# A DiT block on one core: four instead of five groups of scale columns, two of them placed inside their K step, and batch 1's layer-norm statistics swapped between two engines

## The chip, the cores and the metric

The kernel runs on one core of one Trainium2 chip. The metric is device microseconds of one execution, the median of several. Names used: PE is TensorE, DVE is VectorE, ACT is ScalarE, POOL is GpSimd, SP is the engine that issues most loads.

## The reference

Shapes are B = 2, N = 256, D = 1152 and F = 4608, all in bf16.

```python
mod = (silu(c) @ w_mod).reshape(B, 6, 1, D)
shift_a, scale_a, gate_a, shift_m, scale_m, gate_m = [mod[:, i] for i in range(6)]
h = layernorm(x) * (1 + scale_a) + shift_a
q, k, v = split(h @ wqkv)                       # 2 heads of 576
a = softmax(q k^T / sqrt(576)) v @ wo
x = x + gate_a * a
h2 = layernorm(x) * (1 + scale_m) + shift_m
out = x + gate_m * (gelu(h2 @ w_fc1) @ w_fc2)
```

The change touches only the first part: the first layer norm, its scale, and the K projection.

## The kernel before

**Tiles.** The 512 tokens are four tiles of 128 (0 and 1 are batch 0, 2 and 3 are batch 1). D is nine chunks of 128. All weights are loaded once into wide tiles by SP, in the order in which they are used. The instructions of each engine run in the order in which the program writes them: the end of the kernel adds a dependency from each instruction to the one before it on its engine. Eight semaphores are shared in turn by the loads, so that a load waits until the eighth load before it has landed.

**Layer norm of x.** For tiles 1 and 3, DVE computes mean and variance (`stats_piece`, L193 and L195, in three pieces of 384 columns). For tiles 0 and 2, ACT does (`act_stats`, L204: two passes over the tile that sum and sum squares), and small operations on DVE and POOL make mean and variance of the sums (`act_sq_mean` L211, `act_var` L222, `act_mean` L216). The reciprocal root comes from POOL (`pool_rsqrt`, L327) for tiles 0, 1 and 3, and from ACT (`ln_exp_rsqrt`, L227 and L228: Ln, then Exp with scale -0.5) for tile 2. `norm1` (L231, DVE) subtracts and multiplies into `xn`, first columns 0 to 512 (`CUT`), later the rest.

**Chunks and scale.** PE transposes `xn` chunk by chunk into PSUM (`transpose_x`, L262, tile `pt`). `scale_group(k0, k1)` (L245) makes the scales of the chunks k0 to k1 with nine matmuls a chunk of two columns each, out of `w_scale_a`. `scale_add` (L255 on DVE, L253 on ACT) adds 1 and puts them in SBUF. `modulate` multiplies half a chunk (one batch) by its scale and writes it to SBUF, on DVE (L268) or ACT (L270); `both` has DVE do batch 0 and ACT batch 1. Chunk 0 of batch 0 is modulated by L356 with the scale straight from PSUM.

**K projection.** `k_step(k)` (L278) runs chunk k of h against six column blocks of `w_k` (m from 0 to 5), each into its own PSUM bank; with `c0, c1` on one batch alone, with `m0, m1` on some of the blocks. The steps 0 to 2 are done by halves, with the preparation of the next chunks between them. From step 3 on, the loop is

```python
for k in range(3, KD):
    if k in (3, 5, 7):
        k1 = min(k + 3, KD)
        scale_add(scale_group(k + 1, k1), k + 1, k1)
    if k < KD - 1:
        both(transpose_x([k + 1], range(NT)), k + 1)
    k_step(k)
```

After it come the last three column blocks (`k_panel`, L307), the shift, Q, attention, the output projection and the MLP, none of which changes. `warm` (L173) and `fill` (L321) are matmuls on zeros that nothing reads.

**Loads.** `SGROUPS` names the groups of scale columns. SP loads x in four loads (tiles 0, 1, 3, 2: L86), then for each group its scale columns (L107) and the rows of `w_k` for the same chunks (L104), and then the other columns of `w_k`, the shift columns and the rest.

Of the kernel before, what the change touches and what calls it, by code (L numbers as in the profile page):

```python
# [9 lines left out]
BF16 = mybir.dt.bfloat16  # L10
ACT = mybir.ActivationFunctionType
# [4 lines left out]
LN_EPS = 1e-5  # L16
# [3 lines left out]
def kernel(  # L20
# [11 lines left out]
    nc = tc.nc  # L32
    B, N, D = x.shape
# [3 lines left out]
    P = 128  # L37
    T = B * N
    NT = T // P
    TPB = N // P  # L40
    KD = D // P
# [18 lines left out]
    def acc_tile(shape, name, dt=FP32):  # L60
        return psum.tile(shape, dt, name=name, tag="acc", bufs=6)

    def aux_tile(shape, name, dt=FP32):
        return psum.tile(shape, dt, name=name, tag="aux", bufs=2)
# [27 lines left out]
    eps_t = const.tile([P, 1], FP32, name="eps_t")  # L92
# [2 lines left out]
    sT = act.tile([P, KD, SW], BF16, name="sT")  # L95
    nc.gpsimd.memset(sT[:], 0.0)

    SGROUPS = [(0, 2), (2, 4), (4, 6), (6, 8), (8, 9)]
    KM1 = 6
    w_scale_a = wide_tile("w_scale_a")  # L100
    w_k = wide_tile("w_k")
# [1 line left out]
    def load_k(k0, k1, c0, c1):  # L103
        nc.sync.dma_start(w_k[:, k0:k1, c0:c1], wqkv_v[:, k0:k1, D + c0:D + c1])  # L104

    for k0, k1 in SGROUPS:
        nc.sync.dma_start(  # L107
            w_scale_a[:, :, k0 * P:k1 * P],
            wmod_v[:, :, S_SCALE_A * D + k0 * P:S_SCALE_A * D + k1 * P],
        )  # L110
        for a, z in [(0, 1), (1, 2)] if k0 == 0 else [(k0, k1)]:
            load_k(a, z, 0, KM1 * P)
    load_k(0, KD, KM1 * P, D)

    first_load = {}
# [29 lines left out]
    hT0 = aT  # L145
# [41 lines left out]
    mv1 = small.tile([P, NT, 2], FP32, name="mv1", tag="mv1", bufs=1)  # L187
    rstd1 = small.tile([P, NT], FP32, name="rstd1", tag="rstd1", bufs=1)
# [3 lines left out]
    def stats_piece(t, j):  # L192
        nc.vector.bn_stats(stats1[t][:, j, :], x_sb[:, t, j * PW:(j + 1) * PW])  # L193
        if j == NPD - 1:
            nc.vector.bn_aggr(mv1[:, t, :], stats1[t][:].rearrange("p a b -> p (a b)"))  # L195
# [3 lines left out]
    dsq = small.tile([P, NT], FP32, name="dsq", tag="dsq", bufs=1)  # L199
    dm2 = small.tile([P, NT], FP32, name="dm2", tag="dm2", bufs=1)  # L200

    def act_stats(t):
        for f, dst in ((ACT.Identity, dsum), (ACT.Square, dsq)):
            nc.scalar.activation(  # L204
                xns[t][:], x_sb[:, t, :], f, bias=x_sb[:, t, 0:1], scale=-1.0,
                accum_out=dst[:, t:t + 1],
            )

    def act_sq_mean(t):
        one = slice(t, t + 1)  # L210
        nc.vector.scalar_tensor_tensor(  # L211
            dm2[:, one], dsum[:, one], -1.0 / (D * D), dsum[:, one], op0=ALU.mult, op1=ALU.mult
        )

    def act_mean(t):
        nc.gpsimd.tensor_scalar(  # L216
            mv1[:, t, 0:1], dsum[:, t:t + 1], -1.0 / D, x_sb[:, t, 0:1], op0=ALU.mult, op1=ALU.add
        )

    def act_var(t):  # L220
        one = slice(t, t + 1)
        nc.vector.scalar_tensor_tensor(  # L222
            mv1[:, t, 1:2], dsq[:, one], 1.0 / D, dm2[:, one], op0=ALU.mult, op1=ALU.add
        )

    def ln_exp_rsqrt(dst, var):
        nc.scalar.activation(dst, var, ACT.Ln, bias=eps_t[:], scale=1.0)  # L227
        nc.scalar.activation(dst, dst, ACT.Exp, scale=-0.5)  # L228

    def norm1(t, c0, c1):  # L230
        nc.vector.tensor_scalar(  # L231
            xns[t][:, c0:c1], x_sb[:, t, c0:c1], mv1[:, t, 0:1], rstd1[:, t:t + 1],
            op0=ALU.subtract, op1=ALU.mult,
        )


    scale_a = act.tile([P, KD, B], FP32, name="scale_a")

    def scale_group(k0, k1, tile_of=aux_tile):
        pm = tile_of([P, k1 - k0, B], "pm")  # L240
        for j in range(k0, k1):
            if j == 0:
                nc.tensor.matmul(pm[:, 0, :], ones_row[:], ones_row[:, 0:B], start=True, stop=False)
            for k in range(KD):
                nc.tensor.matmul(  # L245
                    pm[:, j - k0, :], w_scale_a[:, k, j * P:(j + 1) * P], sT[:, k, 0:B],
                    start=(k == 0 and j > 0), stop=(k == KD - 1),
                )
        return pm

    def scale_add(pm, k0, k1, eng="d"):
        if eng == "a":
            nc.scalar.activation(scale_a[:, k0:k1, :], pm[:], ACT.Identity, bias=ones[:])  # L253
        else:
            nc.vector.tensor_scalar_add(scale_a[:, k0:k1, :], pm[:], 1.0)  # L255

    def transpose_x(ks, ts, pt=None, j0=0):
        if pt is None:
            pt = aux_tile([P, len(ks), len(ts) * P], "pt", BF16)
        for j, t in enumerate(ts, j0):  # L260
            for i, k in enumerate(ks):
                nc.tensor.transpose(pt[:, i, j * P:(j + 1) * P], xns[t][:, k * P:(k + 1) * P], ident[:])  # L262
        return pt

    def modulate(pt, i, k, b, j0, eng):
        dst, src, sc = hT0[:, k, b * N:(b + 1) * N], pt[:, i, j0:j0 + N], scale_a[:, k, b:b + 1]
        if eng == "d":
            nc.vector.tensor_scalar_mul(dst, src, sc)  # L268
        else:
            nc.scalar.mul(dst, src, sc)  # L270
# [3 lines left out]
    def k_step(k, c0=0, c1=T, m0=0, m1=KM1):  # L274
        for m in range(m0, m1):
            if k == 0 and c0 == 0:
                pk[m] = acc_tile([P, T], "pk")
            nc.tensor.matmul(  # L278
                pk[m][:, c0:c1], w_k[:, k, m * P:(m + 1) * P], hT0[:, k, c0:c1],
                start=(k == 0 and c0 == 0), stop=(k == KD - 1), skip_group_check=True,  # L280
            )
# [31 lines left out]
    BT = [range(b * TPB, (b + 1) * TPB) for b in range(B)]  # L313

    def both(pt, k):
        for b, e in enumerate("da"):
            modulate(pt, 0, k, b, b * N, e)

    def fill(n):
        for _ in range(n):  # L320
            nc.tensor.matmul(pwarm[:], zeros[:, 0:P], zeros[:], start=True, stop=True)  # L321

    def pool_eps(t):
        nc.gpsimd.tensor_scalar_add(mv1[:, t, 1:2], mv1[:, t, 1:2], LN_EPS)

    def pool_rsqrt(t0, t1):
        nc.gpsimd.tensor_tensor(  # L327
            rstd1[:, t0:t1], mv1[:, t0:t1, 1:2].rearrange("p t o -> p (t o)"),
            neg_half[:, 0:t1 - t0], op=ALU.pow,
        )  # L330

    warm(8, pwarm)
    act_stats(0)
    act_stats(2)
    for j in range(NPD):
        stats_piece(1, j)
    act_sq_mean(0)
    nc.gpsimd.tensor_scalar_add(dm2[:, 0:1], dm2[:, 0:1], LN_EPS)
    pool_eps(1)
    stats_piece(3, 0)  # L340
    act_var(0)
    pool_rsqrt(0, 2)
    act_mean(0)
    stats_piece(3, 1)
    stats_piece(3, 2)
    pool_eps(3)
    pool_rsqrt(3, 4)
    norm1(1, 0, CUT)
    norm1(0, 0, CUT)
    pt_a = transpose_x([0, 1], BT[0])  # L350
    act_sq_mean(2)
    act_mean(2)
    norm1(3, 0, CUT)
    pm0, pm1 = [scale_group(k, k + 1, acc_tile) for k in range(2)]
    act_var(2)
    nc.vector.tensor_scalar_mul(hT0[:, 0, 0:N], pt_a[:, 0, :], pm0[:, 0, 0:1])  # L356
    scale_add(pm1, 1, 2, "a")
    modulate(pt_a, 1, 1, 0, 0, "d")
    ln_exp_rsqrt(rstd1[:, 2:3], mv1[:, 2, 1:2])
    nc.scalar.copy(scale_a[:, 0:1, :], pm0[:])  # L360
    norm1(2, 0, CUT)
    fill(1)
    pt_c = aux_tile([P, 2, N], "pt", BF16)
    transpose_x([0, 1], [3], pt_c, 1)
    fill(1)
    k_step(0, 0, N)
    transpose_x([0, 1], [2], pt_c, 0)
    k_step(1, 0, N)
    modulate(pt_c, 0, 0, 1, 0, "d")
    modulate(pt_c, 1, 1, 1, 0, "a")  # L370
# [13 lines left out]
    norm1(3, CUT, D)  # L384
    k_step(2, 0, N)
    k_step(2, N, T)
    for k in range(3, KD):
        if k in (3, 5, 7):
            k1 = min(k + 3, KD)
            scale_add(scale_group(k + 1, k1), k + 1, k1)  # L390
        if k < KD - 1:
            both(transpose_x([k + 1], range(NT)), k + 1)
        k_step(k)
    for m in range(KM1):
        k_evac(m)

# [446 lines left out]
```

## Time and profile before

| | |
|---|---|
| median of 9 runs | 243.92 us (243.48 to 244.48) |
| the profiled execution | 243.75 us, its span 242.0 us |
| PE busy | 236.5 us (98% of the span), 1691 instructions |
| DVE, ACT, POOL busy | 91.4, 59.5 and 28.9 us |
| HBM read | 50.14 MB |
| granted PE clock | full in all slices |
| K step matmuls (L278) | 70 in the trace, 12.9 us |
| scale matmuls (L245) | 81, the first at 9.6 us, the last at 23.1 us |

The page splits the span into 40 slices; PE is busy to nine tenths or more in all but the first two and the last. A chain of waits that is followed back from the last instruction tells which engine's time sets the end. The timeline lists instructions by start and duration, with the idle time before them and what ended it in brackets; matmuls of one line are merged, so that a row "x18" covers eighteen of them. A few matmul records are missing from a trace.

### The profile page before, as it was taken

Reading aid. Unit: us, or ns where it says so; the run is one execution under the profiler, and the core shown is the slowest. Engines: PE = TensorE matmul, PEld = TensorE weight load, DVE = VectorE, ACT = ScalarE, POOL = GpSimd, SP = SyncE. Lnnn points to the kernel's source line nnn. Section 1 sums busy time; section 2 is a strip of 40 time slices with the busy share of each in tenths; the row PEclk is TensorE's granted clock in tenths of the full one; section 3 lists DMA queues with packets and bytes.
Section 4 is the critical chain, followed back from the end, with each engine's and each line's share of the span. In section 5 each row is a group of like instructions: output and inputs, shape, how many; then the busy total and the mean of one; then the engine's idle time right before and its main releaser. Section 6 shows DMA issues by size and latency. Waiting matters only on the chain.

```text
span 242.0 us, 3989 instructions
## 1 busy us (share of the span) xinstructions
PE 236.5 (98%) x1691; PEld 145.3 (60%) x1701; DVE 91.4 (38%) x193; ACT 59.5 (25%) x120; POOL 28.9 (12%) x48
## 2 busy tenths in 40 slices
PE   8899999999999999999999999999999999999994
PEld 5685444466667665888844444444665666566674
DVE  4642442319325678831002999950010000000001
ACT  6632322307215032671422333322000000000000
POOL 2400000001400323200000000001121111111111
PEclk9999999999999999999999999999999999999999
DMA  6999999997599999239999999999200000000000
GB/s 213 327 315 285 377 366 392 389 392 246 105 318 395 390 374 148 48 60 359 389 392 392 340 327 284 276 327 282 98 16 16 20 16 16 20 16 18 29 21 16
DMA packets 48781, 53.29 MB, mean 220 GB/s; under 512 B 9587, under 2 KB 36475, under 8 KB 48763
## 3 DMA queue, kind: packets, MB, share of 16 engines
q1 hardware_dynamic: 41312, 50.14, 62.4%
q10 hardware_dynamic: 6939, 1.71, 4.9%
q0 software_dynamic: 512, 1.19, 1.8%
q8 instruction: 13, 0.21, 0.4%
q14 instruction: 5, 0.04, 0.1%
HBM read 50.14 MB, written 1.19 MB: 212 GB/s over the span
## 4 chain that ended last, share of the span: by engine, by line
PE 94%; DMA 3%; SPq 1%; issue 0%; DVE 0%; ACT 0%; DVEq 0%; ACTq 0%
PE pacc L788 29%; PE pacc L732 29%; PE pacc L679 7%; PE pacc L588 7%; PE pq L510 7%; PE pk L278 5%; DMA w_scale_a<-in_w_mod_dram 3%; PE pk L307 2%; PE pa L628 2%; PE ps_s L545 2%; PE pn L405 2%; PE pm L245 1%; PE pt L262 1%; SPq L86 1%; PE pg L487 0%
## 5 line engine op out<-in xcount | busy, mean ns | idle before, releaser
L732 PE MATMUL pacc<-hT,w_f 128*128 128x256 bf16 (+1 forms) x427 | 70.3, 325 | 0.3
L788 PE MATMUL pacc<-w_f,gT 128*128 128x384 bf16 (+2 forms) x468 | 70.5, 314 | 0.0
L788 PEld LDWEIGHTS <-gT 128*128 128x128 bf16 x468 | 44.4, 98 | 26.2
L732 PEld LDWEIGHTS <-w_f 128*128 128x128 bf16 x432 | 42.2, 98 | 27.6
L794 DVE TENSOR_TENSOR tmp<-pacc,gate 128x384 f32<-128x384 f32 (+2 forms) x13 | 6.9, 527 | 65.6 <-PE pacc L788 57.4
L764 ACT ACTIVATE gT<-pacc 128x512 bf16<-128x512 f32 x24 | 14.3, 597 | 32.7 <-PE pacc L732 32.7
L458 DVE SCALAR_TENSOR_TENSOR part<-w_gate_m,s,part 128x1152 f32<-128x1152 bf16 x16 | 21.4, 1414 | 0.0
L796 POOL TENSOR_TENSOR o_sb<-tmp,x 128x384 bf16<-128x384 f32 (+1 forms) x12 | 11.6, 970 | 54.0 <-DVE tmp L794 54.0
L679 PE MATMUL pacc<-w_o,big 128*128 128x384 bf16 x108 | 17.9, 326 | 0.0
L510 PE MATMUL pq<-hT,w_q 128*128 128x512 bf16 x79 | 17.7, 379 | 0.1
L588 PE MATMUL pacc<-w_v,hT 128*128 128x384 bf16 x108 | 17.7, 326 | 0.0
L588 PEld LDWEIGHTS <-hT 128*128 128x128 bf16 x108 | 10.5, 98 | 7.1 <-issue 0.3
L679 PEld LDWEIGHTS <-big 128*128 128x128 bf16 x108 | 10.4, 98 | 7.2 <-issue 0.4
L510 PEld LDWEIGHTS <-w_q 128*128 128x128 bf16 x81 | 7.9, 98 | 9.4
L278 PE MATMUL pk<-big,w_k 128*128 128x256 bf16 (+1 forms) x70 | 12.9, 324 | 0.1
L685 POOL TENSOR_TENSOR x<-tmp,x_sb 128x384 f32<-128x384 f32 x8 | 7.3, 912 | 26.8 <-DVE tmp L684 26.8
L456 DVE TENSOR_SCALAR part<-w_gate_m,s 128x1152 f32<-128x1152 bf16 x2 | 1.6, 818 | 22.1 <-DMA w_gate_m<-in_w_mod_dram 22.1
L480 POOL DMA_DIRECT2D gates_dram<-nat_v x2 | 1.1, 534 | 67.7 <-DVE nat_v L478 67.7
L278 PEld LDWEIGHTS <-w_k 128*128 128x128 bf16 x72 | 6.7, 98 | 3.6
L753 ACT ACTIVATE gT<-pacc 128x512 bf16<-128x512 f32 x12 | 6.5, 598 | 9.1 <-PE pacc L732 9.1
L173 PE MATMUL pwarm<-zeros 128*128 128x256 f32 x20 | 7.4, 538 | 1.2 <-DVE eps_t L93 1.2
L501 POOL DMA_DIRECT2D gates_dram<-nat x4 | 2.4, 608 | 50.4 <-DVE nat L498 49.5
(101 smaller groups left out, 165.9 us busy)
## 6 DMA issues: line engine op xcount, KB each, us to landing
w_f<-in_w_fc_dram SPq DMA_DIRECT2D x12, 864.0 KB, 14.8
w_f<-in_w_fc_dram SPq DMA_DIRECT2D x3, 1728.0 KB, 7.7
w_f<-in_w_fc_dram SPq DMA_DIRECT2D x2, 2592.0 KB, 17.2
w_gate_a<-in_w_mod_dram SPq DMA_DIRECT2D x3, 864.0 KB, 12.1
w_v<-in_wqkv_dram SPq DMA_DIRECT2D x3, 864.0 KB, 13.8
w_o<-in_wo_dram SPq DMA_DIRECT2D x3, 864.0 KB, 14.0
w_shift_m<-in_w_mod_dram SPq DMA_DIRECT2D x3, 864.0 KB, 8.5
w_scale_m<-in_w_mod_dram SPq DMA_DIRECT2D x3, 864.0 KB, 14.2
```

The source lines that it names most:

```text
L173: nc.tensor.matmul(dst[:, 0:T // 2], zeros32[:, 0:P], zeros32, start=True, stop=True)
L278: nc.tensor.matmul(pk[m][:, c0:c1], w_k[:, k, m * P:(m + 1) * P], hT0[:, k, c0:c1], start=(k == 0 and c0 == 0), stop=(k == KD - 1), skip_g ...
L458: nc.vector.scalar_tensor_tensor(part[:, b, :], wg[:, k, :], s32[:, k, b:b + 1], part[:, b, :], op0=ALU.mult, op1=ALU.add,)
L510: nc.tensor.matmul(pq[m][:], w_q[:, k, m * P:(m + 1) * P], hT[:, k, :], start=(k == 0), stop=(k == KD - 1), skip_group_check=True,)
L588: nc.tensor.matmul(pacc[:], hT[:, k, t * P:(t + 1) * P], w_v[:, k, pnl * PW:(pnl + 1) * PW], start=(k == 0), stop=(k == KD - 1),)
L679: nc.tensor.matmul(pacc[:], aT[:, k, t * P:(t + 1) * P], w_o[:, k, c0:c1], start=(k == 0), stop=(k == KD - 1),)
L685: (nc.gpsimd if pool_add else nc.vector).tensor_tensor(x1[:, t, c0:c1], tmp[:], x_sb[:, t, c0:c1], op=ALU.add)
L732: nc.tensor.matmul(dst, w_f1[m // KD][:, k, ml * P:(ml + 1) * P], hT[:, k, c0:c1], start=start, stop=(k == KD - 1), **kw,)
L764: nc.scalar.activation(gT[:, m, :], pacc[:], ACT.Gelu_apprx_tanh)
L788: nc.tensor.matmul(pacc[:], gT[:, kk, t * P:(t + 1) * P], w_f2[j][:, r, c0 - n * PW:c0 - n * PW + cw], start=(kk == 0), stop=(kk == KF - 1),)
L794: nc.vector.tensor_tensor(tmp[:], pacc[:], gate_m[:, b, c0:c0 + cw], op=ALU.mult)
L796: (nc.vector if last else nc.gpsimd).tensor_tensor(o_sb[:], tmp[:], x1[:, t, c0:c0 + cw], op=ALU.add)
```

## The change

There are four groups of scale columns instead of five: chunks (0, 1), (2, 3), (4, 5, 6) and (7, 8). Each row of `w_k` (its first 768 columns) is a load of its own. ACT makes the statistics of tile 3 and DVE those of tile 2; the reciprocal roots of both come from ACT, by an Ln for each and one Exp for the two. Chunk 0 of batch 0 is modulated before tiles 2 and 3 are normalised, chunk 1 of batch 0 on ACT instead of DVE, and the copy of chunk 0's scale runs on DVE instead of ACT. One of the two `fill` matmuls goes, and the four transposes of batch 1's chunks 0 and 1 stand together behind the first half step. In the loop, step 3 runs two of its six matmuls, then the transposes of chunk 4, then the scale matmuls of chunk 4, then the other four; step 4 runs three, the transposes, the scale matmuls of chunks 5 and 6, and three; step 6 runs two, the transposes, those of chunks 7 and 8, and four. The steps 5 and 7 have no group. x is in four loads before and after.

```diff
--- before.py
+++ after.py
@@ -95,7 +95,7 @@
     sT = act.tile([P, KD, SW], BF16, name="sT")
     nc.gpsimd.memset(sT[:], 0.0)
 
-    SGROUPS = [(0, 2), (2, 4), (4, 6), (6, 8), (8, 9)]
+    SGROUPS = [(0, 2), (2, 4), (4, 7), (7, 9)]
     KM1 = 6
     w_scale_a = wide_tile("w_scale_a")
     w_k = wide_tile("w_k")
@@ -108,8 +108,8 @@
             w_scale_a[:, :, k0 * P:k1 * P],
             wmod_v[:, :, S_SCALE_A * D + k0 * P:S_SCALE_A * D + k1 * P],
         )
-        for a, z in [(0, 1), (1, 2)] if k0 == 0 else [(k0, k1)]:
-            load_k(a, z, 0, KM1 * P)
+        for a in range(k0, k1):
+            load_k(a, a + 1, 0, KM1 * P)
     load_k(0, KD, KM1 * P, D)
 
     first_load = {}
@@ -331,40 +331,37 @@
 
     warm(8, pwarm)
     act_stats(0)
-    act_stats(2)
+    act_stats(3)
     for j in range(NPD):
         stats_piece(1, j)
     act_sq_mean(0)
     nc.gpsimd.tensor_scalar_add(dm2[:, 0:1], dm2[:, 0:1], LN_EPS)
     pool_eps(1)
-    stats_piece(3, 0)
     act_var(0)
     pool_rsqrt(0, 2)
     act_mean(0)
-    stats_piece(3, 1)
-    stats_piece(3, 2)
-    pool_eps(3)
-    pool_rsqrt(3, 4)
+    stats_piece(2, 0)
+    stats_piece(2, 1)
     norm1(1, 0, CUT)
     norm1(0, 0, CUT)
     pt_a = transpose_x([0, 1], BT[0])
-    act_sq_mean(2)
-    act_mean(2)
+    act_sq_mean(3)
+    nc.gpsimd.tensor_scalar_add(dm2[:, 3:4], dm2[:, 3:4], LN_EPS)
+    act_mean(3)
+    stats_piece(2, 2)
+    nc.scalar.activation(rstd1[:, 3:4], dsq[:, 3:4], ACT.Ln, bias=dm2[:, 3:4], scale=1.0 / D)
+    nc.scalar.activation(rstd1[:, 2:3], mv1[:, 2, 1:2], ACT.Ln, bias=eps_t[:], scale=1.0)
+    nc.scalar.activation(rstd1[:, 2:4], rstd1[:, 2:4], ACT.Exp, scale=-0.5)
+    pm0, pm1 = [scale_group(k, k + 1, acc_tile) for k in range(2)]
+    nc.vector.tensor_scalar_mul(hT0[:, 0, 0:N], pt_a[:, 0, :], pm0[:, 0, 0:1])
+    nc.vector.tensor_copy(scale_a[:, 0:1, :], pm0[:])
+    scale_add(pm1, 1, 2, "a")
+    modulate(pt_a, 1, 1, 0, 0, "a")
     norm1(3, 0, CUT)
-    pm0, pm1 = [scale_group(k, k + 1, acc_tile) for k in range(2)]
-    act_var(2)
-    nc.vector.tensor_scalar_mul(hT0[:, 0, 0:N], pt_a[:, 0, :], pm0[:, 0, 0:1])
-    scale_add(pm1, 1, 2, "a")
-    modulate(pt_a, 1, 1, 0, 0, "d")
-    ln_exp_rsqrt(rstd1[:, 2:3], mv1[:, 2, 1:2])
-    nc.scalar.copy(scale_a[:, 0:1, :], pm0[:])
     norm1(2, 0, CUT)
     fill(1)
-    pt_c = aux_tile([P, 2, N], "pt", BF16)
-    transpose_x([0, 1], [3], pt_c, 1)
-    fill(1)
     k_step(0, 0, N)
-    transpose_x([0, 1], [2], pt_c, 0)
+    pt_c = transpose_x([0, 1], BT[1])
     k_step(1, 0, N)
     modulate(pt_c, 0, 0, 1, 0, "d")
     modulate(pt_c, 1, 1, 1, 0, "a")
@@ -384,13 +381,16 @@
     norm1(3, CUT, D)
     k_step(2, 0, N)
     k_step(2, N, T)
+    INSIDE = {3: (2, (4, 5)), 4: (3, (5, 7)), 6: (2, (7, 9))}
     for k in range(3, KD):
-        if k in (3, 5, 7):
-            k1 = min(k + 3, KD)
-            scale_add(scale_group(k + 1, k1), k + 1, k1)
-        if k < KD - 1:
-            both(transpose_x([k + 1], range(NT)), k + 1)
-        k_step(k)
+        cut, group = INSIDE.get(k, (0, None))
+        k_step(k, 0, T, 0, cut)
+        pt = transpose_x([k + 1], range(NT)) if k < KD - 1 else None
+        if group:
+            scale_add(scale_group(*group), *group)
+        if pt is not None:
+            both(pt, k + 1)
+        k_step(k, 0, T, cut)
     for m in range(KM1):
         k_evac(m)
```

## The prediction

> **What bounds the kernel now.** I read the chain of waits first, then TensorE's own waits in the first 60 us, then the timeline of the first 26 us, and last ScalarE's waits in the first 30 us. The chain (page, part 4), its shares by engine:
>
> ```profile
> PE 94%; DMA 3%; SPq 1%; issue 0%; DVE 0%; ACT 0%; DVEq 0%; ACTq 0%
> ```
>
> The DMA and SPq shares are the wait for the first group of scale columns, at the start. Everything after it is TensorE. Its waits in 0 to 60 us confirm that:
>
> ```profile
> PE pwarm L173 <- DVE eps_t L93: 1.2, 1, 1.2
> PE pm L245 <- DMA w_scale_a<-in_w_mod_dram: 0.5, 1, 0.5
> ```
>
> After the second one (it ends at 9.62 us) TensorE never stands still for longer than the 0.05 us pieces that the chain calls issue. So a tenth of a microsecond that the change makes TensorE wait, or saves it, moves the end by the same tenth. All of the change lies before 26 us. Two places matter. The first is the start, in the timeline:
>
> ```profile
> 7.41 1.26 ACT L204 ACTIVATE xn<-x_sb 128x1152 bf16<-128x1152 bf16 x1 [1.05 <-DMA x_sb<-in_x_dram]
> 7.79 0.67 DVE L231 TENSOR_SCALAR xn<-x_sb,mv,rstd 128x512 bf16<-128x512 bf16 x2
> 10.25 0.35 DVE L356 TENSOR_SCALAR big<-pt,pm 128x256 bf16<-128x256 bf16 x1
> 10.65 0.81 PE L278 MATMUL pk<-big,w_k 128*128 128x256 bf16 x6
> 11.10 0.41 DVE L231 TENSOR_SCALAR xn<-x_sb,mv,rstd 128x512 bf16<-128x512 bf16 x1
> 11.57 0.29 PE L262 MATMUL pt<-ident,xn 128*128 128x128 bf16 x2
> ```
>
> Tile 2 of x lands last (7.36). Its statistics, its rstd and its normalisation end at 11.51, TensorE transposes it at 11.57, and from there on it has no gap. The second place is one K step with a scale group, here step 3:
>
> ```profile
> 15.88 0.59 PE L245 MATMUL pm<-sT,w_scale_a 128*128 128x2 bf16 x18
> 16.33 0.38 PE L262 MATMUL pt<-ident,xn 128*128 128x128 bf16 x4
> 16.51 0.16 DVE L255 TENSOR_SCALAR scale_a<-pm 128x4 f32<-128x4 f32 x1 [1.03 <-PE pm L245]
> 16.77 1.24 PE L278 MATMUL pk<-big,w_k 128*128 128x512 bf16 x5
> 16.78 0.35 DVE L268 TENSOR_SCALAR big<-pt,scale_a 128x256 bf16<-128x256 bf16 x1
> 17.16 0.47 ACT L270 ACTIVATE big<-pt,scale_a 128x256 bf16<-128x256 bf16 x1 [1.53 <-DVE big L268]
> 17.85 0.39 PE L262 MATMUL pt<-ident,xn 128*128 128x128 bf16 x4
> 18.07 0.38 PE L278 MATMUL pk<-big,w_k 128*128 128x512 bf16 x1
> ```
>
> The reader is to see that the chunk for step 4 is ready at 17.63 (17.16 + 0.47), while TensorE is busy with step 3 and with the next transposes until 18.07. The cover of 0.44 us hides the whole chain from scale group to modulated chunk. ScalarE's half begins only when VectorE's has ended (16.78 + 0.35 = 17.13). That is so every time:
>
> ```profile
> ACT big L270 <- DVE big L268: 9.5, 8, 1.5
> ```
>
> **Rates.** From the chain: six matmuls of 512 columns take 1.29 us, so 0.215 each; four transposes 0.22; 18 scale matmuls 0.43, so 0.024 each, and one ends 0.163 after its start. VectorE: scale_add (L255) 0.16, modulation (L268) 0.35. ScalarE: modulation (L270) 0.47. Hand-overs: TensorE to VectorE 0.04 (16.47 to 16.51), VectorE to itself 0.04, VectorE to ScalarE 0.03, either to TensorE 0.05 (10.60 to 10.65).
>
> **The start.** ScalarE takes the statistics of tile 3, landed by 6.05, in place of tile 2: its two passes start at 6.35 and end near 9.1, 1.06 us earlier. VectorE takes tile 2 and must wait for 7.36: two pieces of statistics (1.01, as the pair at 6.58) end at 8.42, the two normalisations of batch 0 (0.67) at 9.09 and not at 8.46. The four transposes follow 0.11 later, from 9.2 to 9.6, just before the scale columns land (9.57), so this delay is covered; 0.1 more and it would show. Then the third piece (0.55) and the aggregate (0.23) end at 9.99. Chunk 0's modulation no longer waits behind act_var(2): it starts when the first nine scale matmuls are done, about 10.05, 0.2 earlier than 10.25, and step 0 starts at about 10.45 instead of 10.65. But the next thing on TensorE is now all four transposes of batch 1, and these wait for: aggregate 9.99, Ln 10.04 to 10.32, Exp 10.35 to 10.55 (durations 0.28 and 0.20 from L227 and L228), the hand-over of 0.10 seen before L231, and two normalisations of 0.33 and 0.41: 11.39. Transposes at 11.44, step 1 at 11.66. Before, step 1 started at 11.69. The removed fill and the earlier chunk 0 thus turn into a gap of about 0.3 us ahead of the transposes. Modulating chunk 1 on ScalarE ends at 11.2 (scale_add at 10.45, 0.26, then 0.47), ahead of 11.66. The copy of pm0 moves from ScalarE to VectorE and delays nothing but tile 3 there, inside the Exp. Sum of the start: 0.03 us gained. Bounds: 0.33 gained if the normalisations were ready when step 0 ends (11.13), 0.15 lost if the delays on VectorE add up.
>
> **The K steps.** The work on TensorE is the same: 81 scale matmuls, the same transposes. What moves is the order. The group now comes behind the first matmuls of its step and behind the transposes, and only the rest of the step stands between it and the next chunk's first use. Counted from the first matmul of each step:
>
> Step 3 (cut 2): 2 matmuls to 0.43, transposes to 0.65, nine scale matmuls to 0.87, four matmuls to 1.73, and then at once step 4, which needs chunk 4. Chunk 4: last scale matmul ends 1.01, scale_add 1.05 to 1.21, VectorE 1.25 to 1.60, ScalarE 1.63 to 2.10, TensorE at 2.15. A stall of 0.42.
>
> Step 4 (cut 3): three matmuls 0.65, transposes 0.87, 18 scale matmuls 1.30, three matmuls 1.95, transposes of chunk 6 2.17, then step 5. Chunk 5: scale matmuls end 1.44, scale_add 1.48 to 1.64, VectorE to 2.03, ScalarE 2.06 to 2.53, TensorE at 2.58. A stall of 0.41.
>
> Step 6 (cut 2): 0.43, 0.65, 18 scale matmuls 1.09, four matmuls 1.95, transposes 2.17. Chunk 7: 1.23, 1.43, 1.82, 2.32, TensorE at 2.37. A stall of 0.19 (rounded).
>
> Steps 5 and 7 hold no group: their chunk is ready about 0.6 before its use. Step 3 itself starts without a group ahead of it, at 15.85; its chunk is ready at 15.68 (15.16 + 0.47 + 0.05): hidden, and with 0.2 of delay it would show. Sum: 1.02 us. If every hand-over were 0.03 shorter it would be 0.7, if longer 1.3.
>
> **The reads of the transposed chunk.** All of this rests on ScalarE waiting for VectorE. The eight rows say so (eight of eight waits, 0.03 after VectorE's end). In the Trainium skill, "PSUM — Partial Sum Buffer", section "PSUM bank collisions raise a hardware error", two engines must not access one bank at once, reads against reads included, and software has to order them. Both halves of a chunk lie in one tile of 128x512 bf16, so the page speaks for the wait to remain; without it the stalls would be 0.03, 0.03 and none.
>
> **Loads.** SP issues the w_k rows one by one and the third scale group as 864 KB. The old third group (576 KB) was issued at 8.31 and took 7.4 to land, so 15.7, needed at 15.88. The w_k rows ahead of it were issued at 5.14 and took 8.6, so 13.74. The group thus took 1.96; half as much again takes 2.94 and lands at 16.68. It is needed at 16.50 (15.85 + 0.65). This wait adds up to 0.18 to the chain of step 3; with the wider rows somewhat quicker, 0.1. I take 0.1, from 0 to 0.4. The Trainium skill, "DMA: Bandwidth & Descriptors", section "Why small descriptors are slow (HBM only)", gives about 3 cycles for each packet on top of 32 bytes per cycle: an estimate of 27 cycles for 768 bytes against 19 for 512, which gives 16.5 and no wait. Row 4 of w_k comes 192 KB later, about 17.3, needed at 18.0. SP's later loads stand in the same order of bytes, and TensorE needs them later than before: nothing there.
>
> **Sum.** -0.03 + 1.02 + 0.1 = +1.09 us. The profiled execution took 243.75 (span 242.0), which gives 244.84; the median of the nine runs is 0.17 higher, so 245.0. About 0.2% (0.49 us) is what a measurement of this kernel can tell from no change.
>
> **Rivals.** (1) The two modulations overlap, or the stalls are otherwise hidden: 0.06 left, the start as above, 243.9 to 244.1. Against it stand eight of eight waits. (2) Faster: the start yields its bound of 0.33 because the aggregate of tile 2 is done by about 9.65 and not 9.99, and the stalls vanish as in (1): 243.6, or 243.3 where the columns also land a little earlier. It decides only where the K steps cost under 0.3. The profile speaks against it: tile 2 lands at 7.36. (3) The 864 KB land 0.5 later than worked out, since eight loads of w_k are issued one by one: 245.5 to 246.
>
> **How the numbers follow.** Forecast 0.79, (1) 0.06, (2) 0.09, (3) 0.06. The forecast's own range is 244.6 to 245.4 (start +-0.2, steps 0.85 to 1.2, load 0 to 0.3). With a part of (1) and (3) I give 244.3 to 245.6. Slower by over 0.2% is forecast and (3), 0.85; within 0.2% is (1), 0.06; faster is (2), 0.09.
>
> **What would show it.** In the profile after: TensorE waits at L278 for ScalarE's modulation in steps 4, 5 and 7, about 0.42, 0.41 and 0.19; ScalarE still starts behind VectorE; transposes of batch 1 near 11.44 with a gap ahead of them; the third group landing near 16.6. Matmuls of steps 4 and 5 without a gap would prove me wrong.

## The result, and the profile after

The changed kernel takes 244.96 us (median of 9 runs, 244.66 to 245.24) against 243.81 us (29 runs) of the kernel before: a ratio of 1.0046, 95% interval 1.0035 to 1.0058, so 1.1 us slower. The profiled execution took 244.95 us with a span of 243.2, against 243.75 and 242.0.

The chain of the page after is no longer TensorE and one load alone. By engine:

```profile
PE 92%; DMA 2%; DVE 2%; issue 1%; ACT 1%; SPq 1%; ACTq 0%; DVEq 0%
```

DVE and ACT are on it now. TensorE's waits in 0 to 60 us show a new one, for ScalarE's modulation, and the wait for the scale columns has gone:

```profile
PE pwarm L173 <- DVE eps_t L93: 1.2, 1, 1.2
PE pk L278 <- ACT big L270: 0.6, 2, 0.3
```

The timeline of the step that was shown before, step 3, into step 4:

```profile
15.79 0.39 PE L262 MATMUL pt<-ident,xn 128*128 128x128 bf16 x4
16.02 0.38 PE L245 MATMUL pm<-sT,w_scale_a 128*128 128x2 bf16 x9
16.25 1.02 PE L278 MATMUL pk<-big,w_k 128*128 128x512 bf16 x4
16.43 0.16 DVE L255 TENSOR_SCALAR scale_a<-pm 128x2 f32<-128x2 f32 x1 [1.47 <-PE pm L245]
16.62 0.35 DVE L268 TENSOR_SCALAR big<-pt,scale_a 128x256 bf16<-128x256 bf16 x1
17.07 0.47 ACT L270 ACTIVATE big<-pt,scale_a 128x256 bf16<-128x256 bf16 x1 [1.96 <-DVE big L268]
17.59 0.81 PE L278 MATMUL pk<-big,w_k 128*128 128x512 bf16 x3 [0.32 <-ACT big L270]
```

The four matmuls behind the group occupy TensorE until 17.11 (16.25 + 4 x 0.215). Step 4 could start there, and starts at 17.59, when the chunk is done: 0.48 us of stall. The bracket says 0.32, since a matmul counts as busy until its result is out. The same view two steps on, and at step 7:

```profile
19.56 0.39 PE L262 MATMUL pt<-ident,xn 128*128 128x128 bf16 x4
19.74 0.47 ACT L270 ACTIVATE big<-pt,scale_a 128x256 bf16<-128x256 bf16 x1 [2.19 <-DVE big L268]
20.26 1.89 PE L278 MATMUL pk<-big,w_k 128*128 128x512 bf16 x7 [0.31 <-ACT big L270]
...
23.48 0.47 ACT L270 ACTIVATE big<-pt,scale_a 128x256 bf16<-128x256 bf16 x1 [2.64 <-DVE big L268]
23.52 0.39 PE L262 MATMUL pt<-ident,xn 128*128 128x128 bf16 x4
...
24.01 2.75 PE L278 MATMUL pk<-big,w_k 128*128 128x512 bf16 x12
```

Four transposes take 0.22 to issue, so TensorE is free at 19.78 and 23.74 and goes on at 20.26 and 24.01: stalls of 0.48 and 0.27. The three make 1.23 us. The start, in the same view:

```profile
7.04 1.02 DVE L193 BATCH_NORM_STATS2 stats<-x_sb 128x6 f32<-128x384 bf16 x2 [0.35 <-DMA x_sb<-in_x_dram]
9.68 0.36 DVE L356 TENSOR_SCALAR big<-pt,pm 128x256 bf16<-128x256 bf16 x1 [0.18 <-PE pm L245]
10.09 0.81 PE L278 MATMUL pk<-big,w_k 128*128 128x256 bf16 x6
10.16 0.73 DVE L231 TENSOR_SCALAR xn<-x_sb,mv,rstd 128x512 bf16<-128x512 bf16 x2
10.96 0.40 PE L262 MATMUL pt<-ident,xn 128*128 128x128 bf16 x4
11.19 1.47 PE L278 MATMUL pk<-big,w_k 128*128 128x256 bf16 x12
```

Step 1 starts at 11.19, 0.50 earlier than the 11.69 of before. But tile 2 of x landed at 6.99 here and at 7.36 there. The gain is mostly an early landing of this one execution (below).

**A measure without the start and the end.** From the first matmul of step 1 to the first of `k_panel` (L307), all these kernels do the same TensorE work. In the profile before that stretch is 11.69 to 25.89, 14.20 us; after it is 11.19 to 26.59, 15.40 us. The stretch alone is longer by the whole 1.20 us by which the two spans differ; the other three terms cancel: -0.50 at the start, +0.14 ahead of the first matmul of the MLP (L732, 217 matmuls in 23.94 instead of 23.80), and +0.36 between the last addition and the end of the span (2.83 instead of 2.47).

The first two differ between executions of one kernel. The start goes with the landing of x. From the first matmul of `k_panel` to the last addition nine of the fourteen profiles take 213.64 us, and five take 0.09 to 0.62 more; in the two longest the profile names a wait of L732 for the tile `hT`.

**The end.** The third term is no scatter. The last addition, and SP's wait for the last store at the end of the kernel (waits of SP from 239 us on), before:

```profile
239.24 0.29 DVE L796 TENSOR_TENSOR o_sb<-tmp,x 128x128 bf16<-128x128 f32 x1
SPq L838 <- DMA out_dram<-o_sb: 0.6, 1, 0.6
```

and after:

```profile
240.08 0.29 DVE L796 TENSOR_TENSOR o_sb<-tmp,x 128x128 bf16<-128x128 f32 x1
SPq L838 <- DMA out_dram<-o_sb: 1.0, 1, 1.0
```

In both, the last store lands 1.47 us after the addition. From that landing to the end of the span it is 0.96 us before and 1.33 after. The kernel ends with a row of waits by which SP makes sure of every transfer, in a fixed order of semaphores, 0.06 us from one wait to the next. The eight semaphores of the loads and stores are used in turn. Before, SP issues 70 transfers, and the last store has a semaphore near the end of that order; after, it issues 72, and the last store has one near the start. Six waits that were over before the landing now come behind it, 6 x 0.06 = 0.36. In the four profiles with the loads of before the end (last addition to end of span, unrounded) takes 2.43 to 2.45 us, in the nine with the loads of after 2.79 to 2.81, and in the one with single rows alone (73 transfers, so five waits more) 2.75. So the price belongs to the number of transfers, and not to the K steps.

### The profile page after: what moved, and what is told of

Its sections match the earlier page's. It is cut to its first block, busy times and chain, and to the rows that moved or that the text cites. A ratio compares the mean times of both kernels' runs of the same rounds, so it can differ in the third digit from the quotient of the medians.

```text
span 243.2 us, 3987 instructions
## 1 busy us (share of the span) xinstructions
PE 237.1 (97%) x1689; PEld 145.4 (60%) x1700; DVE 91.2 (37%) x192; ACT 60.3 (25%) x121; POOL 28.2 (12%) x47
## 3 DMA queue, kind: packets, MB, share of 16 engines
q0 software_dynamic: 512, 1.19, 1.9%
HBM read 50.14 MB, written 1.19 MB: 211 GB/s over the span
## 4 chain that ended last, share of the span: by engine, by line
PE 92%; DMA 2%; DVE 2%; issue 1%; ACT 1%; SPq 1%; ACTq 0%; DVEq 0%
PE pacc L788 29%; PE pacc L732 29%; PE pacc L679 7%; PE pacc L588 7%; PE pq L510 7%; PE pk L278 4%; PE pk L307 2%; DMA x_sb<-in_x_dram 2%; PE pa L628 2%; PE ps_s L545 2%; PE pn L405 2%; PE pt L262 1%; PE pm L245 1%; ACT big L270 1%; DVE xn L231 1%
## 5 line engine op out<-in xcount | busy, mean ns | idle before, releaser
L732 PE MATMUL pacc<-hT,w_f 128*128 128x256 bf16 (+1 forms) x427 | 70.3, 325 | 0.3
L732 PEld LDWEIGHTS <-w_f 128*128 128x128 bf16 x432 | 42.2, 98 | 27.8 <-issue 0.2
L796 POOL TENSOR_TENSOR o_sb<-tmp,x 128x384 bf16<-128x384 f32 (+1 forms) x12 | 11.7, 972 | 54.0 <-DVE tmp L794 54.0
```

Of the source, the lines that this page charges most:

```text
L732: nc.tensor.matmul(dst, w_f1[m // KD][:, k, ml * P:(ml + 1) * P], hT[:, k, c0:c1], start=start, stop=(k == KD - 1), **kw,)
L796: (nc.vector if last else nc.gpsimd).tensor_tensor(o_sb[:], tmp[:], x1[:, t, c0:c0 + cw], op=ALU.add)
```

## The experiments

Each was compared with the kernel before on the same chip. "Stretch" is the one just described, from each run's profile; the stalls should show in it. "End" is what the end takes over the 2.44 us of the profile before, and "sum" adds the two.

| run | stretch, us | over 14.20 | end | sum | ratio of medians (95% interval) | in us |
|---|---|---|---|---|---|---|
| after | 15.40 | 1.20 | 0.36 | 1.56 | 1.0046 (1.0035 to 1.0058) | 1.1 |
| loop alone | 15.42 | 1.22 | 0.36 | 1.58 | 1.0058 (1.0041 to 1.0075) | 1.4 |
| head alone | 14.18 | -0.02 | 0.00 | -0.02 | 1.0000 (0.9984 to 1.0016) | 0.0 |
| cuts at zero | 14.49 | 0.29 | 0.36 | 0.65 | 1.0016 (0.9998 to 1.0034) | 0.4 |
| cuts late | 16.70 | 2.50 | 0.36 | 2.86 | 1.0103 (1.0084 to 1.0122) | 2.5 |
| one engine | see text | 0.34 | 0.37 | 0.71 | 1.0039 (1.0023 to 1.0056) | 1.0 |
| group first | 14.81 | 0.61 | 0.36 | 0.97 | 1.0051 (1.0032 to 1.0069) | 1.2 |
| rows alone | 14.20 | 0.00 | 0.31 | 0.31 | 1.0013 (0.9998 to 1.0028) | 0.3 |
| group first, old start | 14.78 | 0.58 | 0.37 | 0.95 | 1.0037 (1.0021 to 1.0053) | 0.9 |
| one engine, old start | 14.54 | 0.34 | 0.36 | 0.70 | 1.0019 (1.0002 to 1.0036) | 0.5 |
| after again | 15.39 | 1.19 | 0.36 | 1.55 | 1.0066 (1.0043 to 1.0089) | 1.6 |
| head again | 14.19 | -0.01 | -0.01 | -0.02 | 1.0015 (0.9995 to 1.0036) | 0.4 |

Eleven of the twelve sums lie inside the interval of their median. The first row does not: its sum is 0.15 over the upper bound (1.4), and what the start or chance took off there is not settled. The same kernel, run again, has 1.6.

**Which part costs?** The loop with its loads alone, and the start alone:

```diff
 # loop alone: the kernel before, with
-    SGROUPS = [(0, 2), (2, 4), (4, 6), (6, 8), (8, 9)]
+    SGROUPS = [(0, 2), (2, 4), (4, 7), (7, 9)]
 # ... w_k row by row, and the loop of the kernel after
 # head alone: the kernel after, with SGROUPS, the w_k loads and the loop of the kernel before
```

> The kernel before with the new loads and the new K-step loop alone; the start is the old one. Theory (the chain from scale group to modulated chunk is no longer covered): after a group's last matmul the chain takes 0.16 - 0.02 + 0.04 + 0.16 + 0.04 + 0.35 + 0.10 + 0.47 + 0.05 = 1.35 us (0.10 is the hand-over to ScalarE as the profile after shows it), and the cover is 0.86 in step 3, 0.65 + 0.22 in step 4 and 0.86 + 0.22 in step 6, so stalls of 0.49, 0.48 and 0.27: 1.24 over the kernel before. Rival (the new start costs, or the loads do): within 0.3 of the kernel before.

> The kernel before with the new start alone (statistics swapped, chunk 0 first, one fill less); groups, loads and loop are the old ones. Theory: -0.03 against the kernel before, between -0.35 and +0.15. Rival 1 (the start gained 0.5, as the two profiles have it: step 1 starts at 11.19 and not at 11.69): -0.5. Rival 2 (the start costs): +0.3 or more.

The loop alone costs 1.4 us (1.0 to 1.8), with 1.22 in the stretch and 0.36 at the end; the head alone 0.0 (within 0.4). The rival that the start makes the loss falls, and so does the one that the start gained 0.5. The new loads are in the loop's run too; what they cost is told below.

**Does the cover behind a group decide?** The cuts at 0, and later:

```diff
-    INSIDE = {3: (2, (4, 5)), 4: (3, (5, 7)), 6: (2, (7, 9))}
+    INSIDE = {3: (0, (4, 5)), 4: (0, (5, 7)), 6: (0, (7, 9))}   # cuts at zero
+    INSIDE = {3: (4, (4, 5)), 4: (5, (5, 7)), 6: (4, (7, 9))}   # cuts late
```

> The kernel after with the three cuts at 0: all six matmuls of a step stand behind its transposes and its scale matmuls. Theory: the cover is 1.29 + 0.22, more than 1.35, so all three stalls go: 1.24 less than the kernel after, so within 0.1 of the kernel before, or a little under it by what the start gains. Rival (the wider group of 864 KB, or the single rows of w_k): no change against the kernel after, +1.1 over before.

> The kernel after with cuts of 4, 5 and 4 in place of 2, 3 and 2, so two matmuls fewer (0.43) behind each group. Theory: each stall grows by 0.43, to 0.92, 0.91 and 0.70: 2.53 in all, 1.29 over the kernel after, 2.5 over before. Rival (loads): no change against the kernel after, or less, since the group is needed later.

Cuts late: 2.50 in the stretch, as worked out (2.53); the median, 2.5 (2.0 to 3.0), does not tell this from the sum of 2.86. Cuts at zero: the stalls are gone, but 0.29 remains in the stretch, which I had not expected. The timeline of that run names it:

```profile
15.43 0.39 PE L262 MATMUL pt<-ident,xn 128*128 128x128 bf16 x4
15.94 0.29 PEld L245 LDWEIGHTS <-w_scale_a 128*128 128x128 bf16 x9 [0.30 <-DMA w_scale_a<-in_w_mod_dram]
15.94 0.38 PE L245 MATMUL pm<-sT,w_scale_a 128*128 128x2 bf16 x9
```

With no matmuls ahead of it, the group of 864 KB is needed at 15.65 and lands at about 15.9. So the four groups need the first matmuls of step 3 ahead of the scale matmuls, for the load, and by the sums above nearly all of them behind, for the chain (a cut between 0 and 2 was not tried).

**Is it the length of the chain?** Two ways to shorten it, each first with the new start and then with the old one:

```diff
 # one engine
-        for b, e in enumerate("da"):
+        for b, e in enumerate("dd"):
 # group first
-        pt = transpose_x([k + 1], range(NT)) if k < KD - 1 else None
         if group:
             scale_add(scale_group(*group), *group)
+        pt = transpose_x([k + 1], range(NT)) if k < KD - 1 else None
```

> The kernel after, with VectorE doing both halves of a chunk in the loop, one after the other, so that nothing passes from VectorE to ScalarE. Theory (the sum of the chain behind a group decides): 0.35 in place of 0.10 + 0.47, so each chain is 0.22 shorter and the stalls are 0.27, 0.26 and 0.05: 0.58 in all, 0.66 less than the kernel after, 0.5 over before. Rival (ScalarE's wait for VectorE is not what holds TensorE, or VectorE becomes the bound): no change against the kernel after, or slower.

> The kernel after with each group ahead of the transposes of its step instead of behind them, still behind the first matmuls. Theory: the scale is ready 0.22 earlier and the chain then starts at the transposes; ScalarE waits for VectorE alone, so its hand-over is 0.03 and not 0.10 as after. Stalls of 0.27, 0.27 and 0.05, 0.59 in all, and up to 0.1 of waiting for the 864 KB, which are needed 0.22 earlier: 0.5 to 0.65 less than the kernel after. If the hand-over stays 0.10: 0.21 less gain. Rival (it is the transposes or the loads): no change.

In the profiles both theories hold. Group first, the timeline of step 3 (the next chunk is done 0.27 after TensorE is free, and ScalarE starts 0.03 after VectorE's end at 17.62, not 0.10):

```profile
17.27 0.35 DVE L268 TENSOR_SCALAR big<-pt,scale_a 128x256 bf16<-128x256 bf16 x1
17.65 0.47 ACT L270 ACTIVATE big<-pt,scale_a 128x256 bf16<-128x256 bf16 x1 [1.79 <-DVE big L268]
18.82 0.59 PE L245 MATMUL pm<-sT,w_scale_a 128*128 128x2 bf16 x18
```

Its stalls are 0.27, 0.28 and 0.05 (expected 0.27, 0.27, 0.05). With one engine they are 0.17, 0.17 and none: less than the 0.27, 0.26 and 0.05 expected, since two modulations back to back take 0.61 together, not 0.70. But the medians missed: 1.2 and 1.0 over before instead of about 0.6 and 0.5. Of this, the end is 0.36 and 0.37, which the expectations left out. Both profiles also had the start late, with tile 2 of x landing at 7.74 and 7.64, and the longest waits ahead of the MLP (0.34 and 0.62). Both loops were then run on the old start, with the kernel after and the head alone on the same chip:

> The old start with the new loads and loop, each group ahead of its transposes. The run with the new start and this loop showed stalls of 0.27, 0.28 and 0.05 in its profile, yet its median was 1.14 over before. Theory (the stalls are all that the loop costs, and the rest came from the new start, where tile 2 of x landed at 7.74): 0.6 over before. Rival (something else in loop or loads costs 0.5): 1.1 over before.

> The old start with the new loads and loop, VectorE doing both halves. The run with the new start showed stalls of 0.17, 0.17 and 0 in its profile, yet its median was 1.08 over before. Theory: 0.34 over before, or 0.4 with a wait for the 864 KB. Rival (something else costs): 1.0 over before.

> The kernel after once more, on the chip of these runs. Theory: 1.24 of stalls plus what the new start costs here, which the next kernel measures by itself; so 1.1 to 1.3 over before where the start costs nothing, and up to 1.8 where it costs 0.5 as in the two runs that fell short. Its profile shows when tile 2 of x lands.

> The kernel before with the new start alone, once more. Theory: between -0.3 and +0.1 against before, if the landing of tile 2 is only scatter. Rival (the new start costs on some chips): +0.4 or more, and tile 2 lands at 7.6 or later in its profile.

Now the order is as the stalls have it: after 1.6 (1.0 to 2.2), group first 0.9 (0.5 to 1.3), one engine 0.5 (0.05 to 0.9). On the old start, less chain is less time. The sums with the end are 1.55, 0.95 and 0.70, against an expected 0.6 and 0.34 for the last two. Their rival, that something else in loop or loads costs 0.5, was right in part: the loads cost 0.36, at the end of the kernel. With it the two runs on the new start are 0.2 to 0.3 above their sums, inside their intervals. The head alone, at 0.4 this time (-0.1 to 0.9), cannot be told from nothing.

**The other parts.** The single rows of w_k, and the kernel before again for its landing times:

> The kernel before with the rows of w_k loaded one by one, nothing else. Theory: no difference, since no wait for them shows: within 0.2 of before. Rival (more loads cost): slower by 0.4 or more.

> The kernel before once more, for its profile: when tile 2 of x and the first scale columns land. If the landing differs between executions, it is elsewhere than at 7.36 and 9.57 here; if the old start brings it about, it is there again, since the one other profile with the old start had 7.34.

Rows alone: no wait for a row and 0.00 in the stretch, but 0.31 at the end. The median, 0.3 (0.0 to 0.7), agrees with that, and by itself could not be told from nothing. In the kernel before, taken again, ScalarE starts tile 2 at 7.17, so the landing is earlier than the 7.36 above with the same start. Landing times differ between executions: 6.9 to 7.4 in six profiles with the old start, 6.8 to 7.7 in eight with the new. In six of these eight, step 1 starts 4.19 or 4.20 after the landing (among them 6.99 and 11.19, 7.11 and 11.31, 7.25 and 11.45, 7.74 and 11.94); in cuts late it is 4.4, where step 0 waits for the scale columns, and in one engine the clock was lower (last section). With the old start the distance is 4.2 to 4.6. So at one landing the new start is 0 to 0.4 ahead, and the scatter of the landing, 0.9, covers that.

No version here beats the kernel before. The new start with the old loop, the single rows, and cuts at zero are equal to it within the intervals; every placement of a group behind the first matmuls of its step is slower.

## Why the prediction was right

The forecast was 245.0 (244.3 to 245.6) and slower with 0.85; measured 244.96. The cause that it named is there. That the sum, +1.09, comes so close to the measured +1.1 is partly luck. The stalls cost 0.21 more than forecast and the load 0.1 less, and the end of the kernel cost 0.36, for which the sum had no term: of SP's later loads it said "nothing there" and did not count the transfers. The parts as measured make 1.56, which the kernel after shows in its second run (1.6, 1.0 to 2.2) and not in its first (1.1, 0.9 to 1.4). Its steps:

- **The K steps (+1.02).** Right in place, order and cause, and a fifth too small: 0.48, 0.48 and 0.27 were measured against 0.42, 0.41 and 0.19. The mis-sized term is the hand-over from VectorE to ScalarE, taken as 0.03 from the rows of before. There VectorE's own wait for the transposes stood in front, and ScalarE had one wait; after, VectorE no longer needs that wait, and ScalarE has two (for VectorE and for TensorE). It starts 0.10 after VectorE's end (16.97 to 17.07) in all three steps, and 0.03 again in group first, where it has one. The forecast's bound for hand-overs, 1.3, held it. The chain shows the second wait as a piece of its own on ScalarE's sequencer (ACTq), in step 3 of after:

```profile
16.62 0.36 DVE big L268
16.99 0.02 issue
17.01 0.02 ACTq L270
17.02 0.05 issue
17.07 0.48 ACT big L270
```

  and in step 3 of group first, without it:

```profile
17.27 0.36 DVE big L268
17.63 0.02 issue
17.65 0.48 ACT big L270
```

  The rows of before had the price of a second wait too, on VectorE: 0.11 from the end of scale_add (16.67) to the modulation (16.78), against 0.03 after (16.59 to 16.62).
- **The reads one after the other.** ScalarE started after VectorE in every group step of after. That agrees with the rule that the prediction took from the Trainium skill, "PSUM — Partial Sum Buffer", section "PSUM bank collisions raise a hardware error"; whether the same engine pair on two banks would overlap was not tried.
- **The load of 864 KB (+0.1).** Too dear: issued at 8.32, it landed 7.6 later, at 15.9, and was needed at 16.02. No wait. By bytes it should have landed at 16.68. Most of the difference is that the load ahead of it landed at 13.3 and not at the 13.74 taken from before. From landing to landing the 864 KB then took 2.7 us (2.66 to 2.71 in nine profiles), against 1.97 to 2.01 for 576 KB in five: 1.35 times as long for 1.5 times the bytes. So rows of 768 bytes go quicker by the byte than rows of 512. The estimate from the Trainium skill, "DMA: Bandwidth & Descriptors", section "Why small descriptors are slow (HBM only)", has that direction and less of it (27 to 19, 1.42 times). Cuts at zero shows how near a wait was.
- **The start (-0.03).** Right within what can be measured: 0.0 and 0.4, each +-0.4 or 0.5. The working put step 1 at 4.30 behind the landing of tile 2; it is 4.20. The gap ahead of batch 1's transposes is there (step 0's last matmul issues until 10.75, the transposes start at 10.96), and is 0.2 rather than 0.3. One of its readings was too strong: before, too, TensorE stood still for about 0.27 us after 9.62, from the last issue of step 0 (10.65 + 6 x 0.107 = 11.30) to the transposes at 11.57; the busy time hides it, since a matmul counts until its result is out.
- **Rivals.** The overlap of the two modulations: no. A faster start that shows: no. A late load: no; the late landings that were seen are those of x. What the loads did cost, 0.36 at the end, was in no rival.

## What to carry to other kernels

When a preparation is moved into a loop step, add up its whole chain on the other engines, hand-overs included, and compare it with the work that still stands behind it on the bound engine: here 1.35 us of chain against 0.86 to 1.08 of cover. The same work in an earlier place was free. Count the waits that each instruction gets as well: one that moved from VectorE to ScalarE was worth 0.07 us, three times. And look at the end of the kernel, also for a change at its start: two transfers more cost 0.36 us there, by the semaphore that the last store happened to get.

## What the runs showed of the hardware

The granted TensorE clock fell to half for about 3.4 us in one profile. In one engine, TensorE stood still from 7.75 to 9.50, because the transposes of batch 0 came late; from about 11.7 the profile has the clock at half:

```profile
9.50 0.38 PE L262 MATMUL pt<-ident,xn 128*128 128x128 bf16 x4 [1.75 <-DVE dm L211]
...
12.01 2.77 PE L278 MATMUL pk<-big,w_k 128*128 128x256 bf16 x12
```

```profile
11.70:15.00 3.30, 3.30 (x31) 2.55 (x32) 1.06 (x3) 0.47 (x1) 0.00 (x0) 0.50 1.10 337
```

The last line is a stretch of the windows view: start and end, length, busy time and count of PE, PEld, DVE, ACT and POOL, then the clock, 0.50. Twelve matmuls of 256 columns took 2.77 us instead of 1.47. This execution took 246.69 us, against 244.22 to 245.29 for nine of the other ten; its mean clock was 0.991. (The stretch of this run is left out of the table for this reason; its 0.34 are the stalls alone.) That the gap brought the clock down is not shown. A gap of 1.2 us at the same place, in head alone, left it at 1.00, though TensorE was busy for as little of a like stretch there (2.13 us of 7.70 to 11.10) as in one engine ahead of the fall (2.15 us of 8.29 to 11.70). Single executions with a mean clock of 0.993 or less occurred with both starts, the kernel before among them; whether the new start, which leaves TensorE idle for longer there, has more of them was not settled.
